# Three small subtractions ahead of every fifth indirect transfer that GpSimd would issue in a row

## The chip, the cores and the metric

The kernel runs on one core of a Trainium2 chip. The metric is device time in microseconds (us), the median of several runs. The engines are named as in the profile: PE is TensorE (matmuls; PEld its weight loads), DVE is VectorE, ACT is ScalarE, POOL is GpSimd, SP is SyncE, whose queue issues nearly all plain transfers.

## The reference, cut to what matters

```python
def _attn_ref(x, h):                      # x 8 x 5696 x 128, h 5696 x 128
    L = 2 * S
    Yf = np.fft.rfft(x, n=L, axis=1) * np.fft.rfft(h, n=L, axis=0)[None]
    return np.fft.irfft(Yf, n=L, axis=1)[:, :S, :]
...
def _moe_ref(x, modality_id, w_gate, modality_bias, w1, w2):   # x is that result, 45568 x 128
    logits = x @ w_gate + modality_bias[modality_id]           # 8 experts
    e_idx = np.argmax(logits, axis=1)
    ...                                                        # softmax probability of the chosen one
    for e in range(E):
        mask = e_idx == e
        h = np.maximum(x[mask] @ w1[e], 0.0)                   # 128 -> 1024
        out[mask] = gate_w[mask, None] * (h @ w2[e])           # 1024 -> 128
```

It is a long causal convolution along the sequence, for each channel, and then a layer of eight experts of which each token uses one.

## The kernel before, in words

The convolution is done as a transform in two levels, by matmuls with constant matrices, for four groups of two batches each. `stage1` multiplies with the first level's cosines and sines (matmul L552) and stores to DRAM. `stage23` loads that (tile `zb`), does the second level (L620), multiplies with the filter on DVE (`product`, L627), adds on POOL or DVE (`add`, L633 and L634), splits into a high and a low part (`high` on ACT, `low` L640 on DVE or POOL) and goes back (L646 to L652). `stage4` goes back over the first level (L738, L739, L744) and has the tokens as rows in a tile `rt`, of which there are eight (`rt_sl`). In seven chunks for each group it then routes: it turns the rows (L756), computes the logits (L763), picks the expert and the place of every token in a short chain over DVE, PE and ACT (`best`, `counts`, `totals`, `ranks`, `places`, `gates`; L796 to L838), and sends the rows to their expert's part of the DRAM table `rows` by indirect transfers on POOL (`dispatch`, L852), one for each 128 tokens, 8 to 16 in a chunk. `experts` loads tiles of 512 (at the end 256) sorted rows, runs the two layers (`gemm1` L970 to L972, `h_high` on ACT L975, `h_low` on DVE L978, `gemm2` L986 to L988), turns the result (L995), scales it by the gate (L998 on DVE) and scatters it to the output by indirect transfers on POOL (`scatter`, L1002), four for a tile of 512. Helper `copy` (L445 on ACT, L447 on DVE) empties most PSUM banks. The expert tiles begin while later groups are still being transformed, so that PE has work of both kinds; in the last fifth of the span only expert tiles are left.

The order of the instructions on each engine is written by a small planner, class `Plan`. Each piece of work is a `step` with an assumed time on one or several engines, the steps it comes after, and a due time (from the knots in `AIMS`, with a lead for each kind of step). `Plan.run` walks through an assumed timeline: whenever an engine is free it starts, among the steps that are ready, the one with the earliest due time, emits its instructions there and then, and marks the engine busy for the assumed time. A step that may run on either of two engines (`add`, `low`, `drain` and others) goes to the one that takes it first. The chip then runs each engine's instructions in that order as soon as their semaphores allow, at its own pace. The steps with a `lag` are the indirect transfers, `dispatch` and `scatter`; the planner assumes 1.35 us of POOL for each. `BURST` keeps the fifth of them at least 4.97 us behind the first in the assumed timeline, which four of 1.35 us exceed by themselves.

Of the kernel before, what the change touches and what calls it, by code (L numbers as in the profile page):

```python
# [13 lines left out]
F32 = mybir.dt.float32  # L14
# [4 lines left out]
ALU = mybir.AluOpType  # L19
# [116 lines left out]
class Plan:  # L136
# [5 lines left out]
    RATE = 0.30e6  # L142
    ROWS = 58e3
    BURST = 4, 7.13, 4.97

    def __init__(self):
        self.steps = []
        self.part = ""

    def step(self, work, emit, after=(), due=0.0, take=(), free=(), st=None, lag=0.0, nbytes=0, early=None, order=None):  # L150
# [16 lines left out]
    def run(self):  # L167
        ready = {e: [] for e in self.SYNC}
        busy = {e: False for e in ready}
        total = {e: 0.0 for e in ready}  # L170
        events = []
        count = 0
        channel = woken = 0.0
        begun = [-100.0] * self.BURST[0]

# [38 lines left out]
                if all(len(p.idle) >= sum(q is p for q, _ in x.take) for p, _ in x.take):  # L214
                    return x

        now, started = 0.0, 0
        for x in self.steps:
            if not x.left:
                enable(x)  # L220
        while True:
            for e in ready:
                x = None if busy[e] else first(e)
                if x is None:
                    continue
                x.start = now
                started += 1
                for p, key in x.take:
                    x.st[key] = p.take()
                for o in x.work:  # L230
                    ready[o].remove((x.due, x.n, x))
                x.emit(e)
                busy[e] = True
                total[e] += x.work[e]
                end = now + x.work[e]
                push(end, "idle", (e, x))
                if x.lag:
                    begun.append(now)
                    channel = max(channel, now) + self.ROWS / self.RATE
                if x.bytes:  # L240
                    channel = max(channel, end) + x.bytes / self.RATE
                    end = channel + self.LAND
                    push(end, "same", x)
                else:
                    push(end if len(x.work) == 1 else end + self.SYNC[e], "same", x)
                push(end + x.lag, "done", x)
                push(end + x.lag + self.SYNC[e], "next", x)
            if not events:
                break
            now = events[0][0]  # L250
            while events and events[0][0] <= now:
                _, _, kind, x = heapq.heappop(events)
# [16 lines left out]
def conv_moe(  # L269
# [5 lines left out]
    nc = tc.nc  # L275
# [97 lines left out]

    padt = cp.tile([128, RW], F32, name="padt")
    nc.gpsimd.memset(padt, 0.0)
    nc.gpsimd.memset(padt[:, D + 1:].bitcast(I32), OOB_TOK)
    pads = padt.unsqueeze(1).to_broadcast([128, NSUB, RW])

# [121 lines left out]
    def switch(_):  # L500
# [15 lines left out]
        gw_first.idle += [y.rearrange("p (n i k) -> p n i k", n=2, i=2) for y in (x[:, :256], x[:, 256:])]  # L516
        yt_first.idle += of_sl.idle
    ctx.enter_context(tc.manual_schedule())

    def two(t):  # L520
        return t.rearrange("p (i c) -> p i c", i=2)
# [673 lines left out]
```

## Time and profile before

| | us |
|---|---|
| runs of the kernel before | 2453.53, 2447.63, 2449.81 |
| median | 2449.81 |
| the profiled execution | 2456.72 |
| its span, first to last instruction | 2454.7 |

The profile is one execution. Its rows give, for each engine, what ran when, and what ended the idle time ahead of it: "<-issue" means that the engine waited for nothing that the profile shows, "<-remote" that a semaphore was raised at that moment and no instruction of the core had ended there that would have raised it. PE is busy for 2144.5 us of the span (87%), DVE for 1481.0, ACT for 1178.3 and POOL for 1189.2. Until about 300 us the stages of the convolution run alone. The four groups' routing, with the dispatches, lies at about 327 to 540, 606 to 875, 1143 to 1443 and 1668 to 1990 us; after that the remaining expert tiles run to the end. The granted clock of TensorE is given as a share of its upper level: 1.0 is 2.4 GHz and 0.5 is 1.2 GHz, and it averages 0.926.

### The profile page before, as it was taken

How to read it: one execution, taken by the hardware profiler on the slowest of the kernel's cores; microseconds unless marked ns; L12 is line 12 of the kernel's file. 1: busy time of each engine (PE TensorE's matmuls, PEld its weight loads, DVE VectorE, ACT ScalarE, POOL GpSimd, SP SyncE). 2: the span in 40 equal slices, each digit the busy share in tenths (PEclk: the TensorE clock that was granted, in tenths of full speed). 3: DMA queues.
4: the chain of work that ended last, by engine and by line, in shares of the span. 5: the costliest groups of instructions: out<-in, count | busy, mean ns of one | idle time of the engine just before them, and what ended most of it. 6: DMA issues, size and time to landing. Idle time of an engine off the chain costs nothing.

```text
span 2454.7 us, 37648 instructions
## 1 busy us (share of the span) xinstructions
PE 2144.5 (87%) x11166; PEld 1779.7 (73%) x11166; DVE 1481.0 (60%) x2851; ACT 1178.3 (48%) x2392; POOL 1189.2 (48%) x1276
## 2 busy tenths in 40 slices
PE   5699878679775889999879889999788989999997
PEld 4578767557664667777767768887667768888897
DVE  5389645568333569975446679975354455555554
ACT  5556533335432456655445445565344344444443
POOL 2058543456445367854444566654445543333332
PEclk8899988889888999999988999999888999999999
DMA  8999887677765778964444435653323142121630
GB/s 290 292 311 322 262 260 232 219 236 234 238 183 181 221 236 260 302 226 160 145 144 142 141 106 171 203 176 105 97 72 121 58 116 74 48 78 44 248 104 26
DMA packets 236492, 434.69 MB, mean 177 GB/s; under 512 B 37318, under 2 KB 103850, under 8 KB 231681
## 3 DMA queue, kind: packets, MB, share of 16 engines
q1 hardware_dynamic: 212608, 384.15, 50.4%
q0 software_dynamic: 23680, 48.15, 5.8%
q8 instruction: 89, 1.46, 0.2%
q14 instruction: 115, 0.93, 0.1%
HBM read 408.11 MB, written 176.22 MB: 238 GB/s over the span
## 4 chain that ended last, share of the span: by engine, by line
PE 47%; issue 24%; POOL 7%; DMA 7%; another core or an unknown queue 6%; DVE 4%; ACT 2%; SPq 1%; POOLq 0%; ACTq 0%; DVEq 0%
PE bank L620 7%; POOL out L1002 4%; PE bank L972 3%; PE bank L970 3%; PE bank L552 3%; PE bank L986 3%; PE bank L971 3%; PE bank L744 3%; PE bank L987 3%; PE bank L988 3%; PE pl L763 2%; DMA zb<-z 2%; POOL rows L852 2%; DMA raw<-in_w 2%
## 5 line engine op out<-in xcount | busy, mean ns | idle before, releaser
L978 DVE SCALAR_TENSOR_TENSOR hl<-bank,hh 128x512 fp32r<-128x512 f32 x740 | 502.0, 687 | 384.8 <-ACT hh L975 239.5
L975 ACT ACTIVATE hh<-bank 128x512 fp32r<-128x512 f32 x740 | 439.3, 599 | 524.6 <-PE bank L972 309.4
L1002 POOL DMA_INDIRECT out<-of,mrt x370 | 369.0, 997 | 568.7 <-DVE of L998 425.7
L852 POOL DMA_INDIRECT rows<-rt,idx x360 | 358.7, 996 | 229.5 <-issue 127.7
L986 PE MATMUL bank<-hh,slot 128*128 128x512 f32 (+1 forms) x736 | 307.6, 418 | 22.0 <-ACT hh L975 10.9
L627 DVE TENSOR_TENSOR t<-bank,hs 96x512 f32<-96x512 f32 x418 | 264.7, 678 | 102.2 <-remote 40.0
L970 PE MATMUL bank<-mxh,slot 128*128 128x512 f32 (+1 forms) x736 | 308.2, 419 | 14.6 <-issue 8.8
L987 PE MATMUL bank<-hl,slot 128*128 128x512 f32 (+1 forms) x736 | 288.4, 392 | 2.8 <-DVE hl L978 1.7
L972 PE MATMUL bank<-mxh,slot 128*128 128x512 f32 (+1 forms) x736 | 287.7, 391 | 1.0 <-issue 1.0
L971 PE MATMUL bank<-mxl,slot 128*128 128x512 f32 (+1 forms) x736 | 287.9, 391 | 0.8 <-issue 0.7
L988 PE MATMUL bank<-hh,slot 128*128 128x512 f32 (+1 forms) x736 | 286.7, 390 | 0.6 <-issue 0.6
L620 PE MATMUL bank<-zb,m 96*96 96x256 f32 x896 | 236.3, 392 | 21.5 <-DMA zb<-z 10.8
L552 PE MATMUL bank<-xt,ft 128*128 128x256 f32 x540 | 151.8, 420 | 69.6 <-ACT z L445 27.2
L620 PEld LDWEIGHTS bank<-zb,m 96*96 96x96 f32 x896 | 146.7, 168 | 71.4 <-DVE hl L978 7.9
L445 ACT COPY ut<-bank 90x512 f32<-90x512 f32 x209 | 119.8, 581 | 132.2 <-remote 53.1
L633 POOL TENSOR_TENSOR t<-t,t 96x256 f32<-96x256 f32 x117 | 91.3, 781 | 188.7 <-DVE t L627 139.4
L986 PEld LDWEIGHTS bank<-hh,slot 128*128 128x128 f32 x736 | 143.1, 194 | 47.9 <-ACT hh L975 13.1
L970 PEld LDWEIGHTS bank<-mxh,slot 128*128 128x128 f32 x736 | 144.1, 196 | 43.9 <-issue 11.7
L552 PEld LDWEIGHTS bank<-xt,ft 128*128 128x128 f32 x540 | 108.7, 210 | 91.8 <-issue 32.0
L972 PEld LDWEIGHTS bank<-mxh,slot 128*128 128x128 f32 x736 | 142.9, 194 | 31.1 <-issue 0.8
L988 PEld LDWEIGHTS bank<-hh,slot 128*128 128x128 f32 x736 | 142.2, 193 | 29.7 <-issue 1.1
L987 PEld LDWEIGHTS bank<-hl,slot 128*128 128x128 f32 x736 | 143.1, 194 | 27.9 <-DVE hl L978 7.1
(226 smaller groups left out, 4110.3 us busy)
## 6 DMA issues: line engine op xcount, KB each, us to landing
slot<-weights SPq DMA_DIRECT2D x156, 1024.0 KB
z<-z SPq DMA_DIRECT2D x180, 256.0 KB
uu<-u SPq DMA_DIRECT2D x159, 256.0 KB
zb<-z SPq DMA_DIRECT2D x112, 360.0 KB
u<-ut SPq DMA_DIRECT2D x112, 360.0 KB
raw<-in_w SPq DMA_DIRECT2D x88, 256.0 KB
mrt<-rows SPq DMA_DIRECT2D x81, 260.0 KB
hs<-hd SPq DMA_DIRECT2D x96, 192.0 KB
```

Of the source, the lines that this page charges most:

```text
L552: nc.tensor.matmul(two(zt["ps"])[:, t], st["ft"][:, j, 2 * t:2 * t + 2, :], st["xt"][:, j], start=True, stop=True)
L620: nc.tensor.matmul(two(st["px"])[:KP, h], mm, both["zb"][:, k % 2, 1 - h], start=True, stop=True)
L852: nc.gpsimd.indirect_dma_start(views[count[0] % NVIEW], bass.IndirectOffsetOnAxis(ap=rs["idx"][:, t + c:t + c + 1], axis=0), st["rt"][:, c ...
L970: nc.tensor.matmul(po, w[0][:, fs], xh, start=True, stop=False)
L971: nc.tensor.matmul(po, w[0][:, fs], xl, start=False, stop=False)
L972: nc.tensor.matmul(po, w[1][:, fs], xh, start=False, stop=True)
L975: nc.scalar.activation(hf["hh"], hf["ph"], AF.Relu)
L978: nc.vector.scalar_tensor_tensor(hf["hl"], hf["ph"], 0.0, hf["hh"].bitcast(F32), op0=ALU.max, op1=ALU.subtract)
L986: nc.tensor.matmul(po, w[0][:, fs], hf["hh"][:, cs], start=k == 0, stop=False)
L987: nc.tensor.matmul(po, w[0][:, fs], hf["hl"][:, cs], start=False, stop=False)
L988: nc.tensor.matmul(po, w[1][:, fs], hf["hh"][:, cs], start=False, stop=k == 7)
L1002: nc.gpsimd.indirect_dma_start(oviews[(t * NSUB + c) % NVIEW], bass.IndirectOffsetOnAxis(ap=st["rt"].bitcast(I32)[:, c, D + 1:D + 2], axis=0),
```

## The change

A scratch tile `spread` of 128 partitions and 36 columns is set to zero once. The planner counts the indirect transfers that it has emitted on POOL. Ahead of one that would follow four others it emits three subtractions `spread - spread` on POOL, adds 0.85 us to the assumed time of that step, and counts from zero again. Any other POOL step with an assumed time of 0.6 us or more sets the count to zero too (an `add`, a `low`, the `fence` transfer at L1055); the small copy of token numbers at L751 does not. The subtractions wait for no semaphore. Due times, leads and all other numbers stay as they are.

```diff
     BURST = 4, 7.13, 4.97
+    SPACE = 4, 0.85
...
-        now, started = 0.0, 0
+        now, started, row = 0.0, 0, 0
...
+                work, at = x.work[e], now
+                if e == "POOL" and x.lag:
+                    if row >= self.SPACE[0]:
+                        self.space()
+                        work, at, row = work + self.SPACE[1], now + self.SPACE[1], 0
+                    row += 1
+                elif e == "POOL" and work >= 0.6:
+                    row = 0
                 x.emit(e)
                 busy[e] = True
-                total[e] += x.work[e]
-                end = now + x.work[e]
+                total[e] += work
+                end = now + work
                 push(end, "idle", (e, x))
                 if x.lag:
-                    begun.append(now)
-                    channel = max(channel, now) + self.ROWS / self.RATE
+                    begun.append(at)
+                    channel = max(channel, at) + self.ROWS / self.RATE
...
+    spread = cp.tile([128, 36], F32, name="spread")
+    nc.gpsimd.memset(spread, 0.0)
...
+    def space():
+        for _ in range(3):
+            nc.gpsimd.tensor_tensor(spread, spread, spread, op=ALU.subtract)
+    plan.space = space
```

In the changed program's order on POOL there are 453 of these subtractions, 151 groups of three; 114 groups stand ahead of the last dispatch and 37 behind it. No more than four indirect transfers stand next to each other anywhere. The planner's walk shifts with the added 0.85 us, so the order on the other engines changes in places too: 14 pairs of additions on the tiles `t` move from POOL to DVE, 12 copies of `ot` move from DVE to ACT. The amount of expert work between the routing steps stays close: behind the last routing matmul 401 matmuls of L970 stood in PE's order, now 400.

POOL, the second dispatch row of the first group; `rt` holds the token rows, `idx` their places, and x4 means four equal instructions in a row. Before:

```order
L634 TENSOR_TENSOR t_1071<-t_1071,t_1069 96x256
L852 DMA rows<-rt_1090,idx_1097 369152x130 x4
L852 DMA rows<-rt_1091,idx_1097 369152x130 x4
L852 DMA rows<-rt_1092,idx_1097 369152x130 x4
L852 DMA rows<-rt_1093,idx_1098 369152x130 x4
L852 DMA rows<-rt_1094,idx_1098 369152x130 x4
L852 DMA rows<-rt_1095,idx_1098 369152x130 x4
L751 COPY rt_1093<-tokid 128x4
```

The same place now (lines are 17 further down, and buffers are numbered 2 higher):

```order
L651 TENSOR_TENSOR t_1073<-t_1073,t_1071 96x256
L869 DMA rows<-rt_1092,idx_1099 369152x130 x4
L534 TENSOR_TENSOR spread<-spread 128x36 x3
L869 DMA rows<-rt_1093,idx_1099 369152x130 x4
L534 TENSOR_TENSOR spread<-spread 128x36 x3
L869 DMA rows<-rt_1094,idx_1099 369152x130 x4
L534 TENSOR_TENSOR spread<-spread 128x36 x3
L869 DMA rows<-rt_1095,idx_1100 369152x130 x4
L534 TENSOR_TENSOR spread<-spread 128x36 x3
L869 DMA rows<-rt_1096,idx_1100 369152x130 x4
L534 TENSOR_TENSOR spread<-spread 128x36 x3
L869 DMA rows<-rt_1097,idx_1100 369152x130 x4
```

Twenty-four transfers that stood next to each other now stand in six rows of four, with five groups of subtractions between them.

POOL, in the second group's routing (behind the second fence transfer, near 653 us), where dispatches and an expert tile's scatter (`of`, `mrt`) stand next to each other. Before:

```order
L852 DMA rows<-rt_1095,idx_1097 369152x130 x4
L852 DMA rows<-rt_1088,idx_1097 369152x130 x4
L1002 DMA out<-of_2622,mrt_2607 45568x128 x4
L751 COPY rt_1095<-tokid 128x4
L852 DMA rows<-rt_1089,idx_1098 369152x130 x4
```

Now:

```order
L869 DMA rows<-rt_1097,idx_1099 369152x130 x4
L534 TENSOR_TENSOR spread<-spread 128x36 x3
L869 DMA rows<-rt_1090,idx_1099 369152x130 x4
L534 TENSOR_TENSOR spread<-spread 128x36 x3
L1019 DMA out<-of_2624,mrt_2609 45568x128 x4
L534 TENSOR_TENSOR spread<-spread 128x36 x3
L869 DMA rows<-rt_1091,idx_1100 369152x130 x4
```

A scatter counts as a transfer like a dispatch, so the groups stand on both sides of it; the copy moved to another place.

POOL, the end of the program, where only the scatters of 256-row tiles are left, two for each tile. Before:

```order
L1002 DMA out<-of_2621,mrt_2604 45568x128 x2
L1002 DMA out<-of_2622,mrt_2605 45568x128 x2
L1002 DMA out<-of_2621,mrt_2606 45568x128 x2
L1002 DMA out<-of_2622,mrt_2607 45568x128 x2
L1191 UNCONDITIONAL_BRANCH
```

Now:

```order
L1019 DMA out<-of_2623,mrt_2606 45568x128 x2
L1019 DMA out<-of_2624,mrt_2607 45568x128 x2
L534 TENSOR_TENSOR spread<-spread 128x36 x3
L1019 DMA out<-of_2623,mrt_2608 45568x128 x2
L1019 DMA out<-of_2624,mrt_2609 45568x128 x2
L1208 UNCONDITIONAL_BRANCH
```

One group stands ahead of every second tile's scatter there.

## Rows read from the trace of the kernel before

**Rows 1.** Page: busy time by engine; DMA rate in 40 slices.

```profile
PE 2144.5 (87%) x11166; PEld 1779.7 (73%) x11166; DVE 1481.0 (60%) x2851; ACT 1178.3 (48%) x2392; POOL 1189.2 (48%) x1276
...
GB/s 290 292 311 322 262 260 232 219 236 234 238 183 181 221 236 260 302 226 160 145 144 142 141 106 171 203 176 105 97 72 121 58 116 74 48 78 44 248 104 26
```

**Rows 2.** Windows, POOL rows over four transfers: length, busy by engine, clock, DMA, GB/s.

```profile
core 0: us, PE busy (x) PEld busy (x) DVE busy (x) ACT busy (x) POOL busy (x), PEclk, DMA share, GB/s
...
772.40:796.40 24.00, 2.73 (x9) 1.89 (x8) 3.32 (x7) 2.31 (x5) 16.96 (x17) 0.57 0.20 67
...
sum 670.80, PE 481.58 PEld 379.56 DVE 238.91 ACT 183.78 POOL 466.78; mean PE 12.35 PEld 9.73 DVE 6.13 ACT 4.71 POOL 11.97
```

**Rows 3.** Windows over the POOL rows of exactly four transfers ahead of 2000 us.

```profile
sum 197.50, PE 194.37 PEld 161.67 DVE 151.31 ACT 109.27 POOL 144.88; mean PE 6.94 PEld 5.77 DVE 5.40 ACT 3.90 POOL 5.17
```

**Rows 4.** Windows over the rest of 300 to 2000 us, outside rows 2.

```profile
874.90:1143.40 268.50, 250.59 (x1304) 206.13 (x1305) 222.17 (x350) 164.58 (x330) 175.42 (x184) 0.96 0.79 248
...
1442.20:1668.20 226.00, 222.31 (x1195) 185.31 (x1194) 195.35 (x321) 129.65 (x244) 138.49 (x144) 0.99 0.56 170
...
sum 1029.20, PE 982.01 PEld 816.93 DVE 795.85 ACT 605.39 POOL 436.48; mean PE 25.84 PEld 21.50 DVE 20.94 ACT 15.93 POOL 11.49
```

**Rows 5.** Timeline of PE, 769 to 803: start, length, instruction, idle before and releaser.

```profile
774.54 0.59 PE L739 MATMUL bank<-uu,gw 128*128 128x256 f32 x2
799.08 2.08 PE L552 MATMUL bank<-xt,ft 128*128 128x256 f32 x4 [23.95 <-ACT z L445]
```

**Rows 6.** Timeline of ACT, 770 to 800.

```profile
797.57 0.30 ACT L711 COPY gw<-gs 128x128 f32<-128x128 f32 x1 [16.65 <-remote]
```

**Rows 7.** Timeline of SP's queue, 768 to 800.

```profile
770.61 1.43 SPq L705 DMA_DIRECT2D uu<-u  x2
797.52 0.33 SPq L707 DMA_DIRECT2D gs<-in_gq  x1
```

**Rows 8.** Timeline of POOL, 771 to 795, first and last of eighteen.

```profile
771.32 0.98 POOL L852 DMA_INDIRECT rows<-rt,idx  x1 [0.90 <-DVE sm L836]
...
793.46 0.98 POOL L852 DMA_INDIRECT rows<-rt,idx  x1 [0.30 <-issue]
```

**Rows 9.** Timeline of POOL near 1880, the last of a row of eight.

```profile
1893.74 0.98 POOL L852 DMA_INDIRECT rows<-rt,idx  x1 [0.30 <-issue]
```

**Rows 10.** Timeline of DVE, 1893 to 1898, behind that row.

```profile
1896.23 0.69 DVE L447 COPY ot<-bank 128x512 f32<-128x512 f32 x1 [5.46 <-remote]
```

**Rows 11.** POOL's instructions by line and form: count, busy us, mean ns, idle before.

```profile
L852 POOL DMA_INDIRECT rows<-rt,idx x360 | 358.7, 996 | 229.5 <-issue 127.7 <-DVE rt L838 76.3 <-DVE lg L796 15.0
L640 POOL TENSOR_TENSOR yl<-t,yh 96x512 fp32r<-96x512 f32 x76 | 99.8, 1319 | 63.4 <-ACT yh L637 57.8 <-PE bank L972 3.9 <-PE bank L988 1.4
...
L885 POOL TENSOR_TENSOR pre<-raw,pre 128x256 fp32r<-128x256 f32 x21 | 15.1, 737 | 23.4 <-ACT pre L882 20.2 <-DMA hs<-hd 3.1
...
L751 POOL COPY rt<-tokid 128x4 int32<-128x4 int32 x34 | 8.9, 281 | 0.0
```

**Rows 12.** Timeline of POOL, 650 to 656, a transfer behind a subtraction.

```profile
653.53 1.04 POOL L852 DMA_INDIRECT rows<-rt,idx  x1 [0.16 <-issue]
```

**Rows 13.** Line 634 on DVE: shortest, median and longest in ns.

```profile
L634 DVE TENSOR_TENSOR t<-t,t x97: 407/414/1539, 129.9 to 1604.3; 96x256 f32<-96x256 f32 x97
```

**Rows 14.** Windows over the four groups' routing, and the end.

```profile
327.00:540.00 213.00, 160.54 (x773) 126.47 (x772) 110.74 (x276) 68.13 (x163) 104.60 (x119) 0.84 0.74 228
606.00:875.00 269.00, 202.85 (x972) 167.03 (x970) 108.69 (x299) 103.78 (x254) 130.43 (x133) 0.86 0.67 207
1143.00:1443.00 300.00, 253.94 (x1323) 208.92 (x1322) 166.71 (x365) 138.57 (x293) 150.36 (x156) 0.89 0.45 138
1668.00:1990.00 322.00, 275.07 (x1350) 224.44 (x1349) 160.64 (x371) 135.99 (x280) 161.42 (x164) 0.90 0.28 87
2000.00:2440.00 440.00, 437.99 (x2561) 381.94 (x2560) 242.97 (x382) 213.56 (x381) 143.19 (x147) 1.00 0.29 96
```

**Rows 15.** Waits: who waited for whom, us in total, times, longest.

```profile
ACT hh L975 <- remote: 71.6, 17, 12.9
```

More of the change, by code (lines that the diff above doesn't have):

```diff
@@ L144 @@
     BURST = 4, 7.13, 4.97
+    SPACE = 4, 0.85
     def __init__(self):
         self.steps = []
+        self.space = None
         self.part = ""
```

## The prediction, made before the changed kernel ran

> **What bounds the kernel now.** First I read the page for the busy shares: PE works 2144.5 us of the span, DVE, ACT and POOL about half [rows 1], so PE is the engine to fill, and the question is what stands behind its 310 us of idle time. The start and the end do not hold it: from 2000 us on PE is busy for 437.99 of 440 us at full clock [rows 14]. Between 300 and 2000 us I cut the time at the rows of indirect transfers on POOL (a row: transfers that start within 0.7 us of the end of the one before; two of these meet, 771.32 and the one ahead of it, so the cuts follow each other there), each window from the row's first start to 2 us behind its end. There are 39 rows with more than four transfers, and in their 670.8 us PE is busy for 481.58, that is 72%; DVE and ACT fall to 36% and 27% [rows 2]. There are 28 rows of exactly four ahead of 2000 us, and in their windows PE is busy for 194.37 of 197.5 us, 98% [rows 3]. In all that lies outside the long rows it is 982.01 of 1029.2 us, 95% [rows 4]. So 189 us of PE's idle time lie in long rows, and a row of four costs next to nothing.
>
> Then I looked into the longest case, 772 to 797 us. PE's last matmul ends at 774.54 + 0.59 = 775.13 and the next starts at 799.08 [rows 5]. ACT stands idle for 16.65 us up to 797.57 and SP's queue issues nothing between 772.04 and 797.52, and neither has an instruction ending at that moment that would have released it [rows 6, 7]. POOL meanwhile issues eighteen transfers without a pause, from 771.32 to 793.46 + 0.98 = 794.44 [rows 8]. PE had finished its work 22 us before its readers went on; they went on 3.1 us after POOL's row had ended. DVE shows the same behind a shorter row: POOL's eight end at 1894.72, and DVE's copy of a PSUM bank, idle for 5.46 us, starts at 1896.23, 1.5 us later [rows 9, 10]. I read this as follows: while POOL issues indirect transfers back to back, what PE signals at the end of a matmul reaches the others late, and the more transfers stand in the row, the longer it takes to clear: 1.5 us behind eight, 3.1 behind eighteen, 0.16 us for each further one. ACT, DVE and SP wait for PE's signals, then PE for them.
>
> **The change part by part.** *What it removes.* No row longer than four is left in the order on POOL; 114 groups stand where dispatches still follow, 37 among the last scatters. If PE's signals get through as they do in rows of four, the long windows hold the same 481.58 us of PE's work at the 95% that PE reaches elsewhere: 481.58 / 0.954 = 505 us in place of 671, 166 us less. Two things reach beyond that. The clock falls where PE has been idle: the four routing stretches have 0.84, 0.86, 0.89 and 0.90 where the two clean stretches have 0.96 and 0.99 [rows 4, 14]. Their 892.4 us of PE work (sum of the four) are 783 us in full-clock terms; at 0.95 they would take 824, 68 us less. And the floors: in clean stretches PE does (250.59 x 0.96 + 222.31 x 0.99) / 494.5 = 0.93 us of full-clock work in a us [rows 4]. At that rate the stretches with 135, 174, 226 and 248 us of such work need 145, 188, 243 and 266 us. The first moves 213 x 228 = 48.6 MB; at the 304 GB/s of the first four slices [rows 1] that is 160 us, so loads set its floor. Present lengths less floors: 53 + 81 + 57 + 56 = 247 us, the top of what can come of it.
>
> The bottom is less sure. A dispatch row lies within the chunk's own chain (logits, choice, places, gates, dispatch, then a free `rt` tile), and part of what PE loses there would be lost to that chain anyway. I take two thirds of the 166 us, 111, and 25 of the 68 us of clock, nearer to nothing than to all, since the clean stretches have no routing in them.
>
> *What it adds.* No such subtraction stands in the trace. POOL's two-input operations take 737 ns for 256 columns and 1319 for 512 [rows 11], so 2.27 ns a column and 155 ns fixed; 36 columns make 237 ns, three 0.71 us. Below, without a fixed cost, 36 / 256 of 737 is 104 ns, 0.31 us for three; above, POOL's copy of four columns takes 281 ns, 0.84 us for three. I take 0.71, the value on the line between two operations of the same kind. A transfer starts 0.16 us after such an operation [rows 12] and 0.30 us after a transfer, so the pause grows from 0.30 to 0.87 us: a group adds 0.57 us to POOL (0.17 to 0.70). For 114 groups that is 65 us over four stretches of 1104 us in which POOL is busy for 547 [rows 14], so POOL has room; a chunk of sixteen dispatches ends 1.7 us later. Queued behind are the later dispatches, the scatters, and POOL's additions; who waits are the `rt` tiles, free after a chunk's last dispatch. I put a third of the 65 us on the path, 22, for the chunks in which PE waits for a tile. At the end, PE is busy 437.99 of 440 us while POOL is busy for 143.19 [rows 14]: those 37 groups run while POOL waits for the gate and cost nothing.
>
> *The pause against what it must clear.* Behind four transfers the line through eight and eighteen gives 1.5 - 4 x 0.16 = 0.86 us to clear, and four more bring 0.64. The pause is 0.57 us longer than the usual one. That nearly balances; a small remainder over a chunk's four groups would make sixteen behave like a row of six or eight, not like sixteen. I count this as cleared, with a rival for the other case.
>
> *DVE.* Both inputs of a subtraction lie in SBUF. DVE's addition at line 634, two inputs from SBUF, takes 414 ns in the median but 1539 at worst [rows 13], when POOL is at such an operation. The 453 subtractions hold that way for 107 us; DVE is busy half of the time in the routing stretches, mostly with PSUM sources, and waits there itself. I put nothing on the path for it, 10 us at worst. The Trainium skill (SBUF — State Buffer, Who interferes with whom) states that a DVE instruction with two SBUF inputs contends with a GpSimd instruction that reads SBUF, and that this pair of ports is the only place where engines get in each other's way. With the first half the trace agrees (414 against 1539 ns); the second half speaks against this change and is a rival below.
>
> *What it moves.* Additions go from POOL to DVE and copies from DVE to ACT, some dozen each, on engines that are half idle. The mix of expert and convolution work between the routing steps stays as it was. I cost this at nothing, 20 us either way.
>
> *Sum.* 111 + 25 - 22 = 114, rounded to 110 us, off a profiled span of 2454.7 (2456.72 with the 2 us around it). The profiled execution lies 6.9 us above the median; off the median of 2449.81 it gives **2340 us**.
>
> **The rivals.** *Forecast:* signals get through, 2290 to 2400 us (gains of 50 to 160). 60%.
>
> *The chunk's chain stays the limit.* Then only those waits go that no instruction explains; the largest of these is ACT's first step behind `gemm1`, 71.6 us [rows 15]. Less the 22 us of slower POOL this is 50 us at best, and 15 if a third of it comes back as other waits: 2400 to 2435, in the middle 2415. For it: the chunk's chain is serial. Against it: DVE and ACT, which run that chain, are emptier in long rows than anywhere. 18%.
>
> *The pause is too short (slower).* Place: every dispatch chunk. If 0.57 us do not clear what four transfers leave, the rest builds up from group to group, signals stay behind as now, and each chunk's row lasts longer by its groups. The 65 us of longer rows cost what rows cost now, 28% of PE's time: 18 us, 2468; all of it, if the chunk's end is what counts: 2515. It decides where less than 0.64 us clears with each group; the short end of the subtraction's price, 0.17 us, would do it. Against it: rows of four with the usual surroundings lose 2%. 12%.
>
> *The row is not the cause.* Then ACT, DVE and SP stood still for a reason that lies beside POOL's row, and the change brings only its cost: 0 to 15 us, mostly covered, 2450 to 2460. The Trainium skill's sentence just named (SBUF — State Buffer) would have it so. Against it: 72% in long rows and 98% in rows of four. 5%.
>
> *More than forecast,* below 2290, if clock and signals come back in full: 5%.
>
> **How the numbers follow.** The likeliest case gives 2340. The range from 2285 to 2435 holds the forecast and the chain's case, 78%, and a little of the case below. The forecast's own range is 2290 to 2400. A measurement here tells about 0.2%, 5 us (the three runs lie within 6). Faster by more than that: 60 + 18 + 5 = 83, and a point of the others: 84%. Within it: 4%. Slower: 12%.
>
> **What would show it.** Right: POOL's subtractions last 0.2 to 0.3 us each; in the routing stretches PE's idle time falls by more than half, ACT's and DVE's idle stretches that end without a releaser within POOL's rows are gone or under 1 us, and the clock there rises to 0.92 or more; the end from the last dispatch on keeps its length of about 468 us. Wrong: PE still stops for 5 us or more within groups of four; or it runs through the rows and then waits for `rt` tiles, loads (in the first two stretches) or the chunk's chain; or DVE's additions lengthen and PE waits for `product`.

## The result, and the profile after

The changed kernel takes **2225.51 us** (median of four runs, 2220.59 to 2227.44) where the kernel before takes 2448.72 (four runs beside them, 2438.36 to 2453.53): 0.909 of the time, 95% interval 0.906 to 0.912, a gain of 223 us. The forecast was 110 us of gain and 2340 us, its range ended at 2285. Direction and mechanism held; the size did not, and further runs (below) showed that the size belongs to the chip as much as to the kernel: on another chip the same change made the kernel slower.

Lines of the changed kernel are 17 higher than those of before. The page of the changed kernel: busy time by engine, and the granted clock in 40 slices.

```profile
PE 2065.7 (93%) x11166; PEld 1737.1 (78%) x11166; DVE 1496.1 (67%) x2878; ACT 1187.3 (53%) x2408; POOL 1291.6 (58%) x1687
...
PEclk8889999989999989899999999999999899999999
```

Against [rows 1], PE's idle time falls from 310 to 159 us (2224.5 - 2065.7), 151 less, and its busy time, for the same matmuls, by 79, since they run at a higher clock (0.966 over the span, 0.926 before). Together that is the whole difference of the two spans, 230 us.

Windows over the changed kernel's rows on POOL, those with pauses of under 2 us counted as one row, if over four transfers, up to 1768 us.

```profile
sum 816.10, PE 774.07 PEld 646.88 DVE 558.73 ACT 446.26 POOL 616.96; mean PE 35.18 PEld 29.40 DVE 25.40 ACT 20.28 POOL 28.04
```

In the rows PE is now busy for 774 of 816 us, 95%, where it was 72% [rows 2]; DVE goes from 36% to 68%, ACT from 27% to 55%. From 300 us to the end of the last dispatch PE was busy for 1452 of 1687 us at a clock of 0.91 before, and is now for 1390 of 1453 at 0.98; this stretch alone is 234 us shorter.

POOL's timeline in the changed kernel, a group of four and the pauses around it: start, length, instruction, idle time before it.

```profile
1743.44 0.92 POOL L534 TENSOR_TENSOR spread<-spread 128x36 f32<-128x36 f32 x3
1744.84 1.00 POOL L1019 DMA_INDIRECT out<-of,mrt  x1 [0.48 <-issue]
1746.14 0.99 POOL L1019 DMA_INDIRECT out<-of,mrt  x1 [0.30 <-issue]
1747.43 0.98 POOL L1019 DMA_INDIRECT out<-of,mrt  x1 [0.30 <-issue]
1748.72 0.98 POOL L869 DMA_INDIRECT rows<-rt,idx  x1 [0.31 <-issue]
1749.71 0.92 POOL L534 TENSOR_TENSOR spread<-spread 128x36 f32<-128x36 f32 x3
1751.12 1.00 POOL L869 DMA_INDIRECT rows<-rt,idx  x1 [0.49 <-issue]
```

The pause is not the 0.87 us of the prediction. Three subtractions take 0.92, and the transfer behind them starts 0.48 us later and not 0.16: from 1749.70 (1748.72 + 0.98) to 1751.12 the pause is 1.42 us. The median of 138 such pauses is 1.47 us, 1.17 more than the usual 0.30.

The largest waits of the changed kernel: who waited for whom, us in total, times, longest.

```profile
ACT hh L992 <- PE bank L989: 288.0, 274, 3.7
POOL out L1019 <- DVE of L1015: 281.6, 48, 22.0
DVE hl L995 <- ACT hh L992: 203.0, 230, 4.9
```

No wait without a releaser is left among the sixty largest, where before ACT's first step behind `gemm1` alone had 71.6 us [rows 15]; that step now waits for PE's matmul itself, 3.7 us at most. The longest wait that is left to PE is at one place: the first tile of the last level. PE's timeline and SP's queue around it:

```profile
1757.81 0.40 PE L1005 MATMUL bank<-hh,slot 128*128 128x512 f32 x1
1780.40 1.12 PE L973 MATMUL bank<-ident,mrt 128*128 128x128 f32 x4 [22.20 <-DMA mrt<-rows]
```

```profile
1755.28 10.14 SPq L1114 DMA_DIRECT2D rows<-padt  x8
...
1775.55 1.60 SPq L951 DMA_DIRECT2D mrt<-rows  x2
```

The last dispatch ends at 1753.4; then SP fills the pads of the last level, and its rows can be read from 1775.55 on. PE has run out of other work by 1758.

### The profile page after: what moved, and what is told of

It reads as the page before. It is cut to its first block, busy times and chain, and to the rows that moved or that the text cites. A ratio compares the mean times of both kernels' runs of the same rounds, so it can differ in the third digit from the quotient of the medians.

```text
span 2224.5 us, 38050 instructions
## 1 busy us (share of the span) xinstructions
PE 2065.7 (93%) x11166; PEld 1737.1 (78%) x11166; DVE 1496.1 (67%) x2878; ACT 1187.3 (53%) x2408; POOL 1291.6 (58%) x1687
## 4 chain that ended last, share of the span: by engine, by line
PE 53%; issue 18%; POOL 10%; DMA 10%; DVE 5%; SPq 2%; ACT 2%; POOLq 0%; DVEq 0%; ACTq 0%
PE bank L637 7%; POOL out L1019 6%; PE bank L987 4%; PE bank L569 4%; PE bank L1003 4%; PE bank L989 4%; PE bank L988 4%; PE bank L1005 4%; PE bank L1004 4%; PE pl L780 3%; PE bank L761 3%; PE bank L755 2%; PE bank L773 2%; DMA zb<-z 2%; PE bank L669 2%
## 5 line engine op out<-in xcount | busy, mean ns | idle before, releaser
L869 POOL DMA_INDIRECT rows<-rt,idx x360 | 363.4, 1009 | 186.9 <-issue 106.5
L987 PE MATMUL bank<-mxh,slot 128*128 128x512 f32 (+1 forms) x736 | 301.2, 409 | 3.7 <-DVE t L644 2.1
L1003 PE MATMUL bank<-hh,slot 128*128 128x512 f32 (+1 forms) x736 | 301.5, 410 | 0.6 <-issue 0.6
L988 PE MATMUL bank<-mxl,slot 128*128 128x512 f32 (+1 forms) x736 | 283.0, 384 | 0.4
L1004 PE MATMUL bank<-hl,slot 128*128 128x512 f32 (+1 forms) x736 | 281.6, 383 | 1.1 <-DVE hl L995 1.0
L989 PE MATMUL bank<-mxh,slot 128*128 128x512 f32 (+1 forms) x736 | 282.4, 384 | 0.0
L1005 PE MATMUL bank<-hh,slot 128*128 128x512 f32 (+1 forms) x736 | 281.4, 382 | 0.0
L987 PEld LDWEIGHTS bank<-mxh,slot 128*128 128x128 f32 x736 | 140.0, 190 | 29.7 <-DVE t L644 2.5
L989 PEld LDWEIGHTS bank<-mxh,slot 128*128 128x128 f32 x736 | 139.7, 190 | 29.2
L1005 PEld LDWEIGHTS bank<-hh,slot 128*128 128x128 f32 x736 | 139.1, 189 | 28.7
L988 PEld LDWEIGHTS bank<-mxl,slot 128*128 128x128 f32 x736 | 140.4, 191 | 24.3 <-DVE mxl L979 0.8
L1003 PEld LDWEIGHTS bank<-hh,slot 128*128 128x128 f32 x736 | 139.9, 190 | 21.8 <-issue 1.4
L569 PE MATMUL bank<-xt,ft 128*128 128x256 f32 x540 | 140.9, 402 | 16.1 <-DMA zb<-z 8.4
L654 ACT CAST yh<-t 96x512 fp32r<-96x512 f32 x145 | 89.1, 619 | 113.7 <-PE bank L668 32.2
```

Of the source, the lines that this page charges most:

```text
L869: nc.gpsimd.indirect_dma_start(views[count[0] % NVIEW], bass.IndirectOffsetOnAxis(ap=rs["idx"][:, t + c:t + c + 1], axis=0), st["rt"][:, c ...
L987: nc.tensor.matmul(po, w[0][:, fs], xh, start=True, stop=False)
L988: nc.tensor.matmul(po, w[0][:, fs], xl, start=False, stop=False)
L989: nc.tensor.matmul(po, w[1][:, fs], xh, start=False, stop=True)
L1003: nc.tensor.matmul(po, w[0][:, fs], hf["hh"][:, cs], start=k == 0, stop=False)
L1004: nc.tensor.matmul(po, w[0][:, fs], hf["hl"][:, cs], start=False, stop=False)
```

## The experiments

The question was what gives the gain: the pauses or the order that the planner makes of their charge; how long a pause has to be; and what the pauses cost. For each kernel I also took from the trace how long after a matmul's end PE's semaphore update comes. Each update that the trace records is set against the last matmul that ended ahead of it and raises a semaphore. Where it is over 0.3 us later I call the time between **held**, and count how much of PE's idle time lies inside held time: 158 us in the kernel before, 3 us in the changed one. The last 13 us of each run, in which PE has nothing left to do, are not counted. The ends of matmuls are modelled by the profile, so held time doesn't part a late signal from a matmul that itself finished late; and on the chips that hold, some updates have no record in the trace (numbers below), so these sums are rough. Five chips were met in these runs; I call them A to E. Which chip the first comparison ran on isn't on record. The first four kernels ran on A.

**The order without the subtractions.**

```diff
     def space():
-        for _ in range(3):
-            nc.gpsimd.tensor_tensor(spread, spread, spread, op=ALU.subtract)
+        pass
```

> The order of the changed kernel to the last instruction (the planner still charges 0.85 us per group of four), without the subtractions themselves. Theory 'pause' (the subtractions let PE's signals through to ACT, DVE and SP; the new order does nothing): the long rows are back, PE is again busy for about 72% of them, and the time goes back to 2430 to 2460 us, the 2449 of before. Theory 'order' (the gain comes from work that the charge moved): about 2225 us, or 10 less because GpSimd has 128 us less to do. In between, each has its share: by every 22 us above 2225, a tenth of the gain is the pause's.

Measured: 2479.81 us, the kernel before on chip A 2475.02, ratio 1.003 (1.000 to 1.006). PE's idle time inside held time is 146 us. The order gives nothing.

**The subtractions in the order of before.**

```diff
-                        work, at, row = work + self.SPACE[1], now + self.SPACE[1], 0
+                        row = 0
```

> The three subtractions stand behind every four transfers in a row, but the planner isn't charged for them, so the rest stands in the order of before. Theory 'pause': 2220 to 2265 us, that is nearly all of the 223 us of gain, less a little because the planned times of GpSimd are now 0.85 us too short per group. Theory 'order': 2449 us plus up to 20 for the added work.

Measured: 2220.10 us, ratio 0.900 (0.896 to 0.904), 2 us of idle time inside held time. The pause alone gives all of the gain.

**One subtraction in place of three.**

```diff
-        for _ in range(3):
+        for _ in range(1):
```

> One subtraction in each pause in place of three, the order as in the changed kernel. The pause behind four transfers falls from 1.40 us (0.92 of subtractions and 0.48 up to the next transfer) to about 0.8. Theory 'clearing by time' (what PE signals needs about 0.9 us of pause behind four transfers, as the prediction's line through rows of eight and eighteen had it): the rest builds up from group to group, stalls of some us come back late in rows of sixteen, and the time lies between 2270 and 2400 us. Rival 'any gap does' (a single instruction other than a transfer is enough to let the signals through): 2215 to 2230 us, the 60 us of GpSimd's time that is saved being off the path.

Measured: 2456.21 us, ratio 0.994 (0.991 to 0.997), 144 us inside held time. Nearly all of the gain is gone, more than either theory had. POOL's timeline of this kernel says why: the pause is not 0.8 us.

```profile
1697.37 0.97 POOL L869 DMA_INDIRECT rows<-rt,idx  x1 [0.31 <-issue]
1698.35 0.26 POOL L534 TENSOR_TENSOR spread<-spread 128x36 f32<-128x36 f32 x1
1698.78 0.99 POOL L869 DMA_INDIRECT rows<-rt,idx  x1 [0.17 <-issue]
```

Behind a single subtraction the transfer starts 0.17 us later, as the prediction had it from [rows 12]; the pause is 0.44 us here and 0.45 in the median, in place of 0.30, and that clears next to nothing. The 0.48 us stands only behind two and more. The waits without a releaser are back:

```profile
ACT hh L992 <- remote: 51.6, 14, 8.1
ACT ut L457 <- remote: 48.1, 8, 11.6
DVE t L644 <- remote: 36.0, 7, 8.7
```

**Six subtractions.** The same line with `range(6)`.

> Six subtractions in each pause, the order as in the changed kernel. GpSimd gets another 0.85 us per group, 114 groups ahead of the last scatters: 97 us over four routing stretches. If a third of GpSimd's added time lies on the path, as the prediction had it, the time is 32 us longer than 2225, about 2257; if GpSimd's lane has room for it, it stays within 5 us of 2225. If three subtractions still left something uncleared, it falls below 2220.

Measured: 2333.28 us, ratio 0.944 (0.942 to 0.947), 2 us inside held time. Nothing more is cleared (three had been enough), and against the changed kernel's 2225.51, on another chip, 108 us are lost, where the prediction's third had let me expect 32. The pause is 2.44 us in the median, 0.97 longer; in 114 groups that makes 111 us. POOL's timeline of this kernel shows one of them, 2.63 us from the end of the transfer at 1695.94:

```profile
1694.85 1.09 POOL L869 DMA_INDIRECT rows<-rt,idx  x1 [0.30 <-issue]
1695.96 2.12 POOL L534 TENSOR_TENSOR spread<-spread 128x36 f32<-128x36 f32 x6
1698.57 0.99 POOL L869 DMA_INDIRECT rows<-rt,idx  x1 [0.48 <-issue]
```

Here a microsecond of POOL's pause is nearly a microsecond at the end. PE's idle time is 238 us, in the changed kernel 159, and its largest waits are for dispatched tiles (45 us), for POOL's additions, which stand behind the row (39), and for DVE's `yl` (26).

The next four ran on chip B, where the kernel before took 2451.27 us. **Memsets in place of subtractions.**

```diff
-        for _ in range(3):
-            nc.gpsimd.tensor_tensor(spread, spread, spread, op=ALU.subtract)
+        for _ in range(14):
+            nc.gpsimd.memset(spread, 0.0)
```

> Fourteen memsets of the scratch of 36 columns in each pause in place of the three subtractions, the order as in the changed kernel. A memset reads nothing from SBUF, so it is no operation with two inputs there; the pause should be 0.9 to 1.5 us long, near the 1.47 of the subtractions. Theory 'time' (only the length of the pause counts, whatever fills it): 2200 to 2250 us. Rival 'it must be a two-input operation': back to 2440 to 2460 us, as with one subtraction. If the subtractions cost DVE something by its additions with two inputs from SBUF, the memsets come out below the 2225 us by up to 10.

Measured: 2408.44 us, ratio 0.979 (0.973 to 0.986). Both theories miss, since the pause came out far longer than I had reckoned; POOL's timeline of this kernel (the first line is a copy of another step):

```profile
1788.26 0.22 POOL L768 COPY rt<-tokid 128x4 int32<-128x4 int32 x1
1788.38 2.58 POOL L534 MEMSET spread<- 128x36 f32 x14
1791.65 0.99 POOL L869 DMA_INDIRECT rows<-rt,idx  x1 [0.69 <-DVE rt L768]
```

The median pause is 3.25 us. Only 2 us of PE's idle time lie inside held time, so a pause filled with an instruction that reads nothing clears as well as one with two inputs. The time is POOL's lane again: 0.81 us more than with six subtractions in 114 groups, 92 us, cost 75 (2408 against 2333, across two chips). DVE's additions with two inputs from SBUF take 407, 415 and 1505 ns (shortest, median, longest), in the changed kernel 408, 415 and 1505, before 407, 414 and 1539 [rows 13]: the medians don't move. In the changed kernel 14 additions of that line overlap a subtraction, at a median of 459 ns, and 108 don't, at 415: under 1 us in all.

**Three subtractions, but behind eight.** A counter of transfers, `since`, beside the planner's `row`, set to zero at a pause and by the other POOL steps that set `row` to zero; the charge stays every four (the core of the edit).

```diff
                     if row >= self.SPACE[0]:
-                        self.space()
+                        if since >= 8:
+                            self.space()
+                            since = 0
...
+                    since += 1
```

> Three subtractions only behind every eight transfers, so rows of sixteen break into two of eight and not into four of four; the order as in the changed kernel. GpSimd saves about 57 pauses ahead of the last scatters, some 67 us. Theory 'the longer the row, the more there is to clear, and a signal given in its second half waits for its end' (in the kernel before, rows of eight cleared 1.5 us behind their end): stalls of 2 to 4 us in each row, 2270 to 2400 us. Rival 'one pause per row of sixteen is as good': below the 2225 us by up to 60, since GpSimd has more time.

Measured: 2336.03 us, ratio 0.948 (0.941 to 0.955), 78 us inside held time. As the first theory had it.

**Two subtractions.** The line with `range(2)`.

> Two subtractions in each pause, the order as in the changed kernel. In the runs so far the transfer behind one subtraction started 0.45 us behind the transfer ahead of it, behind three 1.47 and behind six 2.44, so two should give 1.1 to 1.2 us. In the changed kernel PE's late signals came through 0.64 to 0.99 us behind a group's last transfer (tenth to ninetieth percentile). Theory 'time': 1.1 us clears that, and GpSimd saves 0.33 us in each of 114 groups, 38 us; six subtractions in place of three cost 1.0 us a group and 108 us, so this is worth up to 37 us: 2185 to 2225. Rival 'it takes more than 1.2 us': stalls come back, 2300 to 2450 us.

Measured: 2210.83 us, ratio 0.901 (0.895 to 0.908), pause 1.15 us in the median, 2 us inside held time. It clears as well as three and is 15 us shorter than the changed kernel's 2225.51 (on another chip; again below).

**One subtraction ahead of each transfer** but a row's first. `range(1)`, and `SPACE = 1, 0.2`.

> One subtraction ahead of every transfer but a row's first, in place of three behind every four; the planner is charged 0.2 us for each, nearly what it costs, and its order shifts by little. Between two transfers 0.45 us in place of 0.30, so each four get 0.6 us more, but in no single gap the 0.9 us that PE's signals needed to come through. Theory 'one gap has to be long enough': the rows stall as before, 2440 to 2500 us. Rival 'the sum of the gaps counts' (0.6 us more a four, against 0.15 with one subtraction and 1.17 with three): at least a third of the gain, 2230 to 2380 us.

Measured: 2263.49 us, ratio 0.919 (0.912 to 0.926), 31 us inside held time. The theory that one gap has to be long enough falls. Of 691 gaps with a subtraction 541 are under 0.46 us; and in the 35 rows of more than four transfers whose gaps all stay under 0.7 us, up to 34 transfers long, PE is busy for 92%, where one subtraction behind four had left it at 73%. The runs where PE's signals are held order by the pause's additional time per transfer (median pause less 0.30, over the transfers of a group):

```
pause                 added per transfer   PE idle in held time   ratio to before
none (new order)            0                    146 us              1.003
0.45 us behind four         0.04                 144                 0.994
1.47 us behind eight        0.15                  78                 0.948
0.45 us behind each         0.15                  31                 0.919
1.15 us behind four         0.21                   2                 0.901
1.47 us behind four         0.29                   3                 0.909
2.44 us behind four         0.54                   2                 0.944
3.25 us behind four         0.74                   2                 0.979
```

I read this as follows: each transfer leaves something and each gap takes some of it away; short rows come off better at the same sum (31 against 78 us at 0.15). Of the lengths tried, the best is the shortest that clears. The ratios come from three chips and the first comparison's; how the kernels compare on one chip is settled below for two of them alone.

The next four ran together on chip C. **Fill the pauses with work that is due.** Two subtractions, and the planner takes an addition of the convolution first, if one is ready (the core of the edit):

```diff
+                fill = full and not x.lag and x.work[e] >= 0.6
...
-                    return x
+                    if not (full and x.lag):
+                        return x
+                    held = held or x
+            return held
```

> Two subtractions as in the run with two, but the planner puts an addition of the convolution (0.74 to 1.32 us, work that is due anyway) into the pause where one is ready, and subtractions only where none is. Theory 'GpSimd's lane is on the path' (six subtractions in place of three cost 1.0 us of end per us of pause, fourteen memsets another 0.8, two in place of three gained 0.4): pauses filled with work that has to be done anyway give back part of the 0.85 us of each of 114 groups, 97 us in all; if a third of the groups find an addition and 0.4 of that reaches the end, 13 us: 2185 to 2210. Rival 'the order is what it was tuned for': an addition ahead of a transfer delays dispatch rows, and the time rises to 2215 to 2260 us.

**Two subtractions behind five.** `SPACE = 5, 0.85`.

> Two subtractions behind every five transfers in place of every four: the pause's 0.85 us more spread over five transfers is 0.17 us a transfer. The runs so far order by this number: 0.04 us a transfer (one behind four) stalls as before, 0.15 (one ahead of each, or three behind eight) leaves 31 or 78 us of PE's idle time inside late signals, 0.21 (two behind four) leaves 2. Theory 'each transfer leaves something, each gap clears at a rate': some 5 to 30 us of stalls, little saved on GpSimd, 2205 to 2245 us. Rival 'up to five are harmless, as four are': 2190 to 2215 us, a fifth of the pauses less.

**Two subtractions, and the changed kernel, on one chip.**

> Two subtractions in each pause once more, beside the changed kernel on the same chip: 2205 to 2225 us, 10 to 15 us below the changed kernel, if the difference seen across chips is one of the kernels.

> The changed kernel as it is, three subtractions, for the comparison on one chip: 2215 to 2235 us.

Measured: 2201.65, 2222.80, 2200.90 and 2222.84 us; but the kernel before takes **2171.48 us** on this chip, C (eleven runs, 2166.16 to 2178.63). The change makes it slower here, 1.0235 (1.0215 to 1.0256). And in none of the four traces is there held time but for 14 us at the very end, in which PE has nothing to do. So the changed kernel takes the same time on both kinds of chip, 2225.51 and 2222.84, while the kernel before differs by 277 us. Of the questions that these runs were for: two subtractions are 22 us better than three on one chip (intervals 1.010 to 1.015 and 1.022 to 1.026), where 10 to 15 had been expected; filling pauses with additions, so that 104 of 151 groups of subtractions are left, gives nothing more; and the rule for groups of five couldn't be tested where nothing is held. That run has fewer pauses (117 groups) and still lies 22 us above two-behind-four; I put that down to its order, which no run tests by itself.

**The kernel before, and the order without subtractions, on chip D.**

> The kernel before, with a trace. On the chip of the last four runs it took 2171 us, on the others 2449 to 2475. Theory 'PE's signals are late only on some chips': where its time is near 2171 us, its rows of sixteen transfers are as long as ever, and no signal of PE comes late in them, PE being busy for 95% or more of the long rows; where its time is near 2450 us, PE is busy for some 72% of them and 140 to 160 us of its idle time lie inside late signals. Rival 'the fast chip has faster transfers or a higher clock': the rows are shorter there (below 0.9 us a transfer), or the clock alone makes the difference, with PE's idle time still above 250 us.

> The order of the changed kernel without the subtractions, once more. On a chip where no signal of PE comes late the changed kernel was 51 us longer than the one before: if the pauses are what costs, this one comes out within 10 us of the kernel before; if the new order is, 30 to 50 us above it. On a chip with late signals: again within 0.5% of the kernel before.

Measured: 2458.22 us (one run; thirteen others have a median of 2459.54) and 2452.49, ratio 0.997 (0.994 to 1.001). Held signals once more, 165 and 137 us of PE's idle time. **The same order on chip E,** where the kernel before takes 2170.80 us:

> The order of the changed kernel without the subtractions, with its rows of sixteen, on one more chip. If the kernel before takes some 2171 us there: no late signals of PE in the rows of sixteen, and, by the theory that the pauses cost the 51 us, 2165 to 2185 us for this one; by the theory that the order costs them, 2200 to 2225. If the kernel before takes some 2450 us there: late signals in the rows, and a time within 0.5% of it.

Measured: 2178.33 us, ratio 1.003 (1.001 to 1.005), as the theory that the pauses cost the 51 us had it. This is the run that parts chip from kernel: the same program, with rows of up to 26 transfers without a pause on D and up to 32 on E. Windows over its rows of more than four transfers, as in [rows 2], first on D (39 rows, 462 transfers), then on E (33 rows, 487 transfers):

```profile
sum 668.70, PE 495.92 PEld 393.40 DVE 272.52 ACT 206.18 POOL 463.87; mean PE 12.72 PEld 10.09 DVE 6.99 ACT 5.29 POOL 11.89
```

```profile
sum 693.50, PE 676.98 PEld 568.06 DVE 480.08 ACT 393.77 POOL 503.06; mean PE 20.51 PEld 17.21 DVE 14.55 ACT 11.93 POOL 15.24
```

On D PE is busy for 74% of the rows, on E for 98%; its idle time over the span is 293 and 123 us, so the clock alone doesn't make the difference. The transfers are not faster on E. Two groups of D's page and the same of E's, transfers by line with their mean length:

```profile
L1018 POOL DMA_INDIRECT out<-of,mrt x370 | 368.9, 997 | 608.7 <-DVE of L1014 492.1
L868 POOL DMA_INDIRECT rows<-rt,idx x360 | 360.3, 1001 | 253.4 <-issue 114.3
```

```profile
L1018 POOL DMA_INDIRECT out<-of,mrt x370 | 368.8, 997 | 460.8 <-DVE of L1014 361.0
L868 POOL DMA_INDIRECT rows<-rt,idx x360 | 365.6, 1015 | 191.3 <-issue 92.2
```

997 and 1001 ns on D, 997 and 1015 on E; between them 0.30 us on both. No wait without a releaser stands in E's list; on D the largest is this one:

```profile
ACT hh L991 <- remote: 49.4, 13, 12.0
```

So what holds PE's signals needs two things, a row of transfers and a chip on which it happens: A, B, D and the chip of the first comparison (which showed held time too) have it, E doesn't, and C shows none either, though its traces have no long row without pauses and only the time of the kernel before, 2171 us, speaks for such rows. Whether it is the chip, the core in it or where the program's memory lies, these runs don't part, and that stays open.

The chips differ in one thing more. Where signals are held, updates of all engines are missing from the trace: on D 201 of PE's 2184, 455 of DVE's 2563 and 366 of ACT's 2268 have no record, on E, in the same program, 1, 1 and 2. In the changed kernel it is 397 of PE's in the first comparison and none on C. So the recording of the trace may have a part in the holding; every run here had its span and clock recorded, and none shows what the kernels take without that.

## Why the prediction was right and where it went wrong

*What bounds the kernel: right.* ACT, DVE and SP did wait for signals of PE that POOL's rows held up; runs with the pause alone (0.900) and the order alone (1.003) show it. The rival that the row is not the cause falls on the chips that hold. By the Trainium skill (SBUF — State Buffer, Who interferes with whom) only the shared pair of ports causes contention. The trace of chip E agrees, with PE busy for 98% of the long rows; those of chip D and the first comparison don't, with 74% and 72%.

*What it removes: mis-sized; this is the step that failed.* The forecast put 111 us (two thirds of 166) and 25 (of 68) on removal, 136 in all. Two measurements say what removal is worth without any pause: the kernel before on chips that hold nothing, 2171 against 2449, 278 us; and one order with its long rows on D and E, 2452 against 2178, 274. Both discounts were wrong, and the "top" of 247 was nearer; the 31 us beyond it are not accounted for. The case that came, clock and signals back in full and a time below 2290, had been given 5%. The reason given for the first was that the dispatch chunk's own chain would keep part of the loss. But that chain (ACT's and DVE's steps between PE's matmuls) was itself what the held signals stretched: in the rows DVE's share nearly doubles and ACT's doubles as soon as nothing is held. The clock term was held back because clean stretches have no routing; the routing stretches then ran at the clean stretches' clock. Windows of the changed kernel over the stretches of [rows 14], though the work has moved ahead in them:

```profile
327.00:540.00 213.00, 203.21 (x1019) 162.15 (x1018) 168.27 (x392) 97.71 (x221) 149.75 (x205) 0.97 0.94 294
606.00:875.00 269.00, 245.46 (x1250) 204.20 (x1250) 182.69 (x398) 158.33 (x347) 199.24 (x259) 0.95 0.88 266
1143.00:1443.00 300.00, 291.51 (x1593) 243.66 (x1593) 255.36 (x463) 165.81 (x314) 218.01 (x259) 0.99 0.55 166
1668.00:1990.00 322.00, 298.46 (x1400) 242.57 (x1399) 175.78 (x327) 145.15 (x252) 152.72 (x227) 0.96 0.27 74
```

They have a clock of 0.97, 0.95, 0.99 and 0.96 for 0.84, 0.86, 0.89 and 0.90. A third of the gain is that clock: 79 of the 230 us of span are shorter matmuls.

*What it adds: right share, wrong length.* The subtraction's 237 ns was near (a lone one takes 268 ns in the median), but three take 0.92 us and the next transfer starts 0.48 us behind them: 1.17 us a group and not 0.57, 133 us over 114 groups and not 65. On chips that hold nothing the pauses cost 2222.84 - 2178.33 = 44.5 us (C against E, where the kernel before takes 2171.48 and 2170.80), which is the third that the prediction took, of twice the length. The charge's new order adds 7.5 (2178.33 against 2170.80). So the sum should have been 278 - 44.5 - 7.5 = 226, and 223 were measured; the predicted terms were 136 - 22. The agreement proves little: the three terms add up to 2448.72 - 2222.84, so it says again that the changed kernel takes the same time on both kinds of chip. The share is no constant: from two subtractions to three the end moves by 22 us for 36 us of pause, from three to six by 108 for 111, as PE's other work that covers it runs out.

Of the 41.6 us between the two profiled spans (2221.1 and 2179.5) 31.6 show in PE's idle time, 154.7 us in the changed kernel on C and 123.1 in its order without pauses on E (spans less busy times), and 10 in longer matmuls, at a clock of 0.961 against 0.973. 13.5 of the 31.6 are the wait for the last level's first tile, 23.0 and 9.5 us there, and 9.3 a wait for DVE's `yl` near 768 us; the rest was not followed. The first is a place that the prediction didn't name: it had looked for waits inside the chunks, and this one comes behind the last of them, when POOL's later end finds PE out of other work.

*The pause against what it must clear: the number near, the outcome in part luck.* The prediction had 0.86 us to clear behind four transfers. In the changed kernel late signals come through 0.64 to 0.99 us behind a group's last transfer (tenth to ninetieth percentile). The planned pause of 0.87 would have been at the edge; the real one, 1.47, was not, and nobody had planned that. By the table above the planned 0.57 us more, 0.14 a transfer, lies just under the 0.15 at which 31 to 78 us of idle time stay held. That a pause which clears a part makes long rows behave like shorter ones fits the runs with 0.15 (78 and 31 of 146 us); a pause of 0.45 us behind four, 0.15 longer than the usual one and 0.04 a transfer, clears next to nothing.

*DVE: right,* nothing. *Moves: right,* within the 20 us (the order alone is 5 and 8 us longer on A and E, 7 shorter on D). *The end: right,* 2224.5 - 1753.4 = 471 us from the last dispatch on, 468 before. *The likeliest rival,* that the chunk's chain stays the limit, had 18%, and no part of it was seen.

*Which version is best* depends on the chip. Two subtractions beat the changed kernel on either kind (2210.83 on B; 2200.90 against 2222.84 on C) and the kernel before where signals are held; where they are not, the kernel before is the fastest of all, 2171.

## What to carry to other kernels

Where several engines stand idle with no releaser in the trace, put their gaps against the rows of back-to-back indirect transfers on GpSimd; a gap between groups, just long enough, was worth a tenth of the time here. Take a loss in a serial chain at its full size when the chain's own engines are emptier there than elsewhere: it is then the loss that makes the chain long. And time such a change on more than one chip, since the same edit gave 9% on one and cost 2.4% on another.

## What the runs showed of the hardware that was not expected

- A semaphore update of PE came up to 22 us after its matmul's end, as the profile models that end, while POOL issued eighteen indirect transfers in a row; the recorded updates of DVE and ACT came within 0.1 us, but for one or two of some 2000 each. On chip E such rows, at the same 1.0 us a transfer, held nothing, and on chip C the kernel before takes as short a time (2171 us).
- On the chips that hold, a tenth of PE's updates and about a sixth of DVE's and ACT's have no record in traces of the kernel before and its order; on C and E next to none are missing.
- On GpSimd a lone subtraction of 36 columns makes a pause of 0.45 us between two transfers, two make 1.15, three 1.47, six 2.44: the second one costs more than twice the others, as the transfer starts 0.17 us behind one and 0.48 behind several.
- Fourteen memsets of the same 36 columns, 131 ns each by the profile, made a pause of 3.25 us.
